# Splitting two products of a Fourier stage once more, and letting ScalarE take casts at any time

## The chip, the cores and the metric

The kernel runs on one core of a Trainium2 chip. The metric is the device time in microseconds, as the median of three runs; the kernel before takes 2945.73 us (2944.1 to 2947.97). One more execution was profiled.

## The reference

Two independent layers whose outputs stand side by side in a 2048 x 2048 result:

```
qkv = x @ wqkv                    # x 2048x1024, wqkv 1024x3072, 32 heads of 32
o = softmax(q k^T / sqrt(32)) v   # for every head
left = o @ wo                     # 2048x1024
a, b = x2 @ Wd_re^T, x2 @ Wd_im^T # first Fourier stage, 1024x1024 matrices
right = Ws_re @ a - Ws_im @ b     # second Fourier stage, 2048x2048 matrices
```

Everything is float32.

## The kernel before, in words

**Arithmetic.** A float32 operand of a projection or Fourier matmul is split into a high part, rounded to TensorE's fast format (`fp32r`), and a low part, the rest. A product of two such operands is three matmuls of 128x128 by 128x512: high-high, low-high and high-low. Each of the large products is cut into 2x2 blocks and done with Strassen's scheme (Winograd's form), seven block products instead of eight, at the price of sums of blocks before and after. `ORDER = (1, 2, 6, 7, 5, 3, 4)` numbers the seven.

**Helpers.** `fetch` loads a block (SyncE issues the DMA) and makes the sums of blocks. `halves` makes the two parts: the cast that makes the high part (line 523 on VectorE, line 522 on ScalarE) and the subtraction that makes the low part (line 526, GpSimd or VectorE). The cast is for VectorE; ScalarE is offered it too only while `spare[0]` is true, which is so in the first five steps of the projection (line 887) and again in the last projection (line 1188), not in attention's time between. `piece` makes a stationary operand, `moving` a moving one. `group` issues the matmuls of one PSUM tile, `gather` reads the finished tile (lines 979 to 1026). An accumulator either stays in SBUF (`Acc`) or travels to HBM and back (`Far`, tiles `x_d`).

**First Fourier stage** (`dense1`). For each of the seven products p there are 8 row blocks i by 2 halves m, and a PSUM tile takes four chunks times three matmuls, 12 in all: 192 matmuls in a product, 1344 in the stage. Rows 0 to 3 accumulate in SBUF, rows 4 to 7 in `x_d`.

**Attention** runs beside these products. For each head, S (line 1317) makes scores for the row maxima: a pair of matmuls into a `psS` tile of 128x1024, VectorE's maximum (line 1323), ScalarE's exponential with sums (line 1326). T (line 1442) makes transposed scores into `psT`, ScalarE's exponential (line 1451) makes `pt`, and V (line 1474) multiplies by the values. `psS` and `psT` have two tiles each.

**Order.** No engine's order is left to a scheduler. `Plan` runs the whole program beforehand with a time for each operation, and writes down an order for each engine. The matmuls of the projections and the Fourier stages ("fills") are one fixed list; S, T and V are three more, and the main loop takes, each time that TensorE is free, the head of one of them by the constants `LATE`, `LEAD`, `STOCK`, `SFIRST` (lines 369 to 378). VectorE, GpSimd, ScalarE and SyncE take what is ready by rank. On the chip each engine then works through its list in order and waits where an input isn't there. The plan lets no GpSimd operation overlap with a VectorE one that has the flag `two`; where a GpSimd operation follows such a one within `Plan.NEAR` (line 79), it is also made to wait for it on the chip.

Of the kernel before, what the change touches and what calls it, by code (L numbers as in the profile page):

```python
# [16 lines left out]
P = 128  # L17
# [48 lines left out]
class Plan:  # L66
# [11 lines left out]
    QUEUE = 1.0  # L78
    NEAR = 0.2

# [140 lines left out]
def kernel(  # L221
# [35 lines left out]
    t2_d = [[dram.tile([P, NB], F32, name=f"t2_d{m}_{k}") for k in range(8)] for m in range(2)]  # L257
    x_d = [[{w: dram.tile([P, NB], F32, name=f"x_d{i}_{m}_{w}") for w in (1, 6, 5)} for m in range(2)] for i in range(4)]
    u4_d = [[dram.tile([P, NB], F32, name=f"u4_d{m}_{i}") for i in range(8)] for m in range(2)]
# [120 lines left out]
    FILL = 3 * (7 * 24 * 4 + 7 * 16 * 4 + 7 * 8 * 16 + 2 * 8 * 4)  # L380
    ATT = H * (128 * MM + 16 * PV) + (3 * H2 + 2 * (H - H2)) * SWITCH
# [81 lines left out]

    def fetch(shape, terms, store=None, keep=None):

        box = {}
        raws, seconds, tile_of, gate = where[0]
        rank = seq()
        sign, *first = terms[0]
        loaded = len(first) == 2  # L470
# [14 lines left out]
        if loaded:  # L485
            last = op("SP", ISSUE, lambda: nc.sync.dma_start(dest(), first[0]), old + first[1] + gate, [users], rank, 256, raws if keep is None else None)
            old = []
        for sign, *term in terms[1:]:
            other = {}
            if len(term) == 2:  # L490
                gold, gusers = seconds.take()

                def load(src=term[0], other=other):
                    other["q"] = tile_of(shape, "g", len(seconds.users))
                    nc.sync.dma_start(other["q"], src)
# [35 lines left out]

    def piece(terms, store=None):

        box = {}
        raw, made, users = fetch([P, 4, P], terms, store)
# [12 lines left out]
        return Piece(h, l, made, both)  # L548
# [9 lines left out]
    def moving(i, terms, store=None, keep=None):  # L558
# [12 lines left out]
        return Piece(h, l, made, mine)  # L571

    whole = lambda t: t

# [41 lines left out]
    def qkv():  # L616
# [269 lines left out]
        for x, (p, blocks, v) in enumerate(STEPS[:10]):  # L886
            spare[0] = x < 5
            if x == 0:
# [67 lines left out]
    def gather(what, X, Y, u3, to, wrote, part=None):  # L956
# [18 lines left out]
        def finish(ps, last):  # L975
# [25 lines left out]
            def put(at, ausers, alast, kind, to, wrote, part):  # L1001
# [20 lines left out]
                if part is not None:  # L1022
                    done = add_op(
                        lambda e: (nc.gpsimd if e == "POOL" else nc.vector).tensor_tensor(out=box["y"], in0=third[0](), in1=box["y"], op=ALU.subtract),
                        [e, third[2]], [users, third[1]], rank)
# [21 lines left out]
    class Far:  # L1047


        def __init__(self, to):  # L1050
            self.to, self.kept, self.last = to, None, None

    FINAL = []
    ab_st = [[[[] for _ in range(NS)] for _ in range(2)] for _ in range(2)]

    def dense1():
# [26 lines left out]
        def load_b(x, n):  # L1083
            p = ORDER[x]
            B[x][n] = moving((8 * x + n) % 12, b_terms(p, n), (t1_d[n], t1[n]) if p == 6 else None)

        B = [[None] * 8 for _ in ORDER]
        for n in range(4):
            load_b(0, n)
        X = {}  # L1090
        for x, p in enumerate(ORDER):
            for i in range(8):
# [19 lines left out]
    def load_ab(step, k):  # L1112
# [10 lines left out]
        }[p]  # L1123
        AB[step, k] = moving((8 * (7 + step) + k) % 12, terms, (t2_d[m][k], t2[m][k]) if p == 6 else None)

    def dense2():
# [3 lines left out]
        for m in range(2):  # L1130
# [13 lines left out]
            for x, p in enumerate(ORDER):  # L1144
                step = 7 * m + x
                for i in range(8):
# [3 lines left out]
                    def terms():  # L1150
                        for k in range(0, 8, 4):
# [4 lines left out]
                            for c in range(4):  # L1156
# [517 lines left out]
```

## Time and profile before

| | |
|---|---|
| median of 3 runs | 2945.73 us |
| profiled execution, whole | 2947.49 us |
| its span, first to last instruction | 2945.7 us |
| TensorE busy, mean granted clock | 2933.7 us, 1.00 |
| VectorE, ScalarE, GpSimd busy | 2300.6, 2271.9, 907.5 us |
| moved by DMA | 588 MB, 200 GB/s |

A matmul's end is modelled, so matmuls overlap in the profile, and a stretch in which TensorE is "busy" can hold waits shorter than a matmul's tail. What one costs is read from a stretch that holds nothing else: its length over the count.

### The profile page before, as it was taken

To read this page: it belongs to the slowest core of one execution; us is meant where nothing else is said; L and a number is where in the kernel's file an instruction comes from. 1 tells how busy PE (TensorE), PEld (TensorE's weight loads), DVE (VectorE), ACT (ScalarE), POOL (GpSimd) and SP (SyncE) were. 2 spreads that over 40 slices of the span, in tenths; PEclk is the share of its full clock that TensorE was granted. 3 is DMA by queue.
4 is the path that set the end of the run, shared out by engine and by line. 5 is a ranking of instruction groups with operands and counts; after the bars stand their busy time and mean duration, and the time that the engine had idled before them with its cause. 6 is when DMAs were issued, how large, how long until landed. Compare 5 with 4: busy or idle time off the path is not lost.

```text
span 2945.7 us, 45665 instructions
## 1 busy us (share of the span) xinstructions
PE 2933.7 (100%) x14922; PEld 2149.6 (73%) x14922; DVE 2300.6 (78%) x3141; ACT 2271.9 (77%) x4321; POOL 907.5 (31%) x709
## 2 busy tenths in 40 slices
PE   9999999999999999999999999999999999999999
PEld 7887777677777777777777777776777766776787
DVE  6778888678877877777678888888777888887685
ACT  4348888888888888888888888888988888886331
POOL 2323336222213332232112543333122444342142
PEclk9999999999999999999999999999999999999999
DMA  9975658667636655665434776565434786655753
GB/s 349 365 237 182 193 184 286 208 214 236 219 109 225 215 177 166 206 231 166 140 111 154 244 230 199 184 195 153 135 112 133 220 264 215 198 179 181 241 201 127
DMA packets 393881, 587.97 MB, mean 200 GB/s; under 512 B 112782, under 2 KB 114574, under 8 KB 393518
## 3 DMA queue, kind: packets, MB, share of 16 engines
q1 hardware_dynamic: 393644, 585.05, 61.8%
q8 instruction: 120, 1.97, 0.3%
q14 instruction: 117, 0.96, 0.1%
HBM read 421.30 MB, written 163.59 MB: 199 GB/s over the span
## 4 chain that ended last, share of the span: by engine, by line
PE 96%; DMA 2%; DVE 1%; SPq 0%; issue 0%; ACT 0%; POOL 0%; DVEq 0%; ACTq 0%
PE pd L416 44%; PE psT L1442 16%; PE psS L1317 16%; PE pd L1474 15%; PE psT L416 6%; DMA qs<-m_d 0%; DVE negm L1323 0%; DMA er<-in_wqk 0%; PE psT L438 0%; DMA g<-in_wqk 0%; DMA raw<-in_wqk 0%; DMA er<-in_xa 0%; DMA g<-in_ct 0%; DMA ks<-qk_d 0%; DVE l L526 0%
## 5 line engine op out<-in xcount | busy, mean ns | idle before, releaser
L1323 DVE TENSOR_REDUCE negm<-psS 128x1 f32<-128x1024 f32 x1024 | 1242.1, 1220 | 239.6 <-PE psS L1317 234.1
L1326 ACT ACTIVATE psS<-psS,negm 128x1024 f32<-128x1024 f32 x1024 | 1219.1, 1190 | 134.3 <-DVE negm L1323 128.7
L416 PE MATMUL pd<-slot,h 128*128 128x512 f32 x3360 | 1147.2, 390 | 0.2 <-DVE ot L1496 0.2
L1451 ACT ACTIVATE pt<-psT 128x512 f32<-128x512 f32 x1296 | 775.0, 695 | 212.5 <-PE psT L1442 201.6
L1442 PE MATMUL psT<-qs,ks 128*128 128x512 f32 x2048 | 793.5, 393 | 1.2 <-DMA qs<-m_d 1.0
L416 PEld LDWEIGHTS pd<-slot,h 128*128 128x128 f32 x3360 | 630.8, 188 | 132.3 <-DVE ot L1496 0.6
L416 PE MATMUL pd<-slot,l 128*128 128x512 f32 x1680 | 654.6, 390 | 0.0
L1317 PE MATMUL psS<-ks,qs 128*128 128x512 f32 x1552 | 473.5, 390 | 1.9 <-ACT psS L1326 1.8
L1442 PEld LDWEIGHTS psT<-qs,ks 128*128 128x128 f32 x2048 | 379.8, 188 | 128.1 <-issue 41.8
L526 POOL TENSOR_TENSOR l<-raw,h 128x512 fp32r<-128x512 f32 x163 | 210.2, 1290 | 728.0 <-PE psT L1442 346.6
L502 POOL TENSOR_TENSOR raw<-raw,g 128x512 f32<-128x512 f32 x225 | 291.9, 1304 | 392.5 <-DVE raw L502 66.2
L416 PEld LDWEIGHTS pd<-slot,l 128*128 128x128 f32 x1680 | 315.4, 188 | 66.8 <-issue 0.8
L1474 PE MATMUL pd<-pt,vt 128*32 128x512 f32 x2592 | 345.8, 594 | 0.4 <-DVE slot L979 0.4
L1317 PEld LDWEIGHTS psS<-ks,qs 128*128 128x128 f32 x1552 | 290.5, 188 | 66.6 <-ACT psS L1326 4.7
L526 POOL TENSOR_TENSOR slot<-raw,slot 128x512 fp32r<-128x512 f32 x174 | 223.8, 1292 | 368.1 <-DVE slot L523 101.5
L1326 ACT ACTIVATION_READ_ACCUMULATOR psS<-psS,negm 128x1 f32 x1024 | 316.6, 309 | 0.0
L1451 ACT ACTIVATE ptm<-psT 128x512 f32<-128x512 f32 x392 | 237.5, 701 | 39.1 <-PE psT L1442 38.4
L1451 ACT ACTIVATE ptl<-psT 128x512 f32<-128x512 f32 x360 | 221.8, 705 | 35.2 <-PE psT L1442 33.2
L1474 PEld LDWEIGHTS pd<-pt,vt 128*32 128x32 f32 x2592 | 89.4, 110 | 180.9 <-issue 173.0
L416 PE MATMUL pd<-slot,slot 128*128 128x512 f32 x768 | 193.7, 390 | 0.0
L416 PEld LDWEIGHTS pd<-slot,slot 128*128 128x128 f32 x768 | 144.2, 188 | 31.0
L523 DVE CAST h<-raw 128x512 fp32r<-128x512 f32 x321 | 148.9, 465 | 16.8 <-PE pd L416 14.2
(138 smaller groups left out, 2362.5 us busy)
## 6 DMA issues: line engine op xcount, KB each, us to landing
raw<-in_ct SPq DMA_DIRECT2D x224, 256.0 KB
g<-in_ct SPq DMA_DIRECT2D x128, 256.0 KB
c<-u_d SPq DMA_DIRECT2D x120, 256.0 KB
qk_d<-e SPq DMA_DIRECT2D x52, 512.0 KB
qs<-qk_d SPq DMA_DIRECT2D x128, 192.0 KB
ks<-qk_d SPq DMA_DIRECT2D x128, 192.0 KB
raw<-ab_d SPq DMA_DIRECT2D x96, 256.0 KB
g<-ab_d SPq DMA_DIRECT2D x80, 256.0 KB
```

Source lines behind the costliest of these rows:

```text
L416: nc.tensor.matmul(box["ps"], a[1]((a[0].hi, a[0].lo)[u]()), b[1]((b[0].hi, b[0].lo)[v]()), start=k == 0, stop=k == n - 1)
L502: return (nc.gpsimd if e == "POOL" else nc.vector).tensor_tensor(out=dest(), in0=dest() if a is None else a.get(), in1=other["q"] if "q" i ...
L523: return nc.vector.tensor_copy(hi(), raw())
L526: return (nc.gpsimd if e == "POOL" else nc.vector).tensor_tensor(out=lo(), in0=raw(), in1=f(hi()), op=ALU.subtract)
L1317: nc.tensor.matmul(p[:, i * NB : i * NB + NB], (QX[0] if own else QS[h % 2])[:, qt * P : qt * P + P], KS[h % 2][:, c * 1024 + i * NB : c * ...
L1323: nc.vector.tensor_reduce(out=ST["negm"][:, c, qt : qt + 1], in_=box["p"], axis=AX.X, op=ALU.max, negate=True)
L1326: nc.scalar.activation(box["p"], box["p"], AF.Exp, bias=ST["negm"][:, c, qt : qt + 1], accum_out=ST["sums"][:, c, qt : qt + 1])
L1442: nc.tensor.matmul(box["p"], KS[h % 2][:, t * P : t * P + P], QS[h % 2][:, j * NB : j * NB + NB], start=True, stop=True)
L1451: nc.scalar.activation(box["t"], box["p"], AF.Exp)
L1474: nc.tensor.matmul(po["p"][j * DH : j * DH + DH, :], VT[h][:, k, :], box["t"], start=(k == t0), stop=(k == t), tile_position=(0, j * DH),)
```

## The change

The products 1 and 2 of the first Fourier stage (`TWICE`) are each split by the same scheme once more: seven products of half the depth, `inner`, in place of eight half-depth ones. The inner sums of blocks are made by `inner_a` and `inner_b`, from the inputs or from tiles kept in HBM (`a2_d`, `b2_d`). The four SBUF accumulators serve the inner products, so all eight rows of the outer ones go through `x_d`. An inner product's stationary operand holds two row blocks by two chunks (`two=True`), its PSUM tile takes 6 matmuls. `turn()` now deals out the 12 slots of moving operands. `spare[0]` is true throughout, and six constants of the plan change.

```
-    NEAR = 0.2            # of Plan
+    NEAR = 0.8
+    b2_d = {p: [dram.tile([P, NB], F32, name=f"b2_d{p}_{c}") for c in range(2)] for p in (1, 2)}
+    a2_d = {p: [dram.tile([P, 4, P], F32, name=f"a2_d{p}_{c}") for c in range(2)] for p in (1, 2)}
+    TWICE, AHEAD = (1, 2), 3
-    LATE = 0.15
+    LATE = 0.05
-    LEAD = 4
+    LEAD = 1
-    STOCK = 1.8
+    STOCK = 1.4
-    SFIRST = 1
+    SFIRST = 0.3
-            spare[0] = x < 5
+            spare[0] = True
...
+        def inner_b(p, q, cc):
+            (sign, at), = OUTER[p][1]
+            r = lambda c2, m: wd[m, 4 * at[0] + 2 * c2 + cc, :, at[1] * NB : at[1] * NB + NB]
+            return {
+                1: lambda: [(1, r(0, 0), [])], 2: lambda: [(1, r(1, 0), [])], 3: lambda: [(1, r(1, 1), [])],
+                5: lambda: [(1, r(0, 1), []), (-1, r(0, 0), [])],
+                6: lambda: [(1, r(1, 1), []), (-1, r(0, 1), []), (1, r(0, 0), [])],
+                7: lambda: [(1, r(1, 1), []), (-1, r(0, 1), [])],
+                4: lambda: [(1, b2_d[p][cc], b2[p][cc]), (-1, r(1, 0), [])],
+            }[q]()
...
+        def inner(x):
+            p = ORDER[x]
+            XI = [a for s in SUMS[:2] for a in accs(s)]
+            YI = [a for s in SUMS[2:] for a in accs(s)]
+            for k, q in enumerate(ORDER):
+                for ip in range(2):
+                    a = piece(inner_a(p, q, ip), (a2_d[p][ip], a2[p][ip]) if q == 6 else None, True)
+                    if ip == 0 and k + AHEAD < 7:
+                        load_inner(x, k + AHEAD)
+                    for il in range(2):
+                        ii = 2 * ip + il
+                        h = DONE.get(q)
+                        to, wrote, part = outer(p, 4 * h[0] + ii, h[1]) if h else (None, None, None)
+                        group(((chunk(a, 2 * il + cc), (B[x][2 * k + cc], whole)) for cc in range(2)), 2, gather(q, XI[ii], YI[ii], None, to, wrote, part))
...
+        for i in range(8):
+            X[i] = [Far(x_d[i][m]) for m in range(2)]
         for x, p in enumerate(ORDER):
+            if p in TWICE:
+                inner(x)
+                continue
```

TensorE's order where product 1 begins. `slot` tiles are moving operands, `h` and `l` a stationary operand's two parts, `pd` PSUM tiles. Before:

```order
L416 MATMUL pd_8889<-slot3_8178,h_8493 128x512
L416 MATMUL pd_8913<-slot4_8600,h_8493 128x512
L1442 MATMUL psT_8923<-qs1_2489,ks1_2490 128x512
L1442 MATMUL psT_8925<-qs1_2489,ks1_2490 128x512
L1317 MATMUL psS_8927<-ks0_530,qx_2491 128x512 x2
L416 MATMUL pd_8913<-slot4_8600,l_8502 128x512
```

The same place after the change:

```order
L419 MATMUL pd_8845<-slot0_7730,h_8506 128x512
L419 MATMUL pd_8845<-slot1_7860,h_8506 128x512
L419 MATMUL pd_8845<-slot1_7860,l_8515 128x512
L419 MATMUL pd_8845<-slot1_7860,h_8506 128x512
L1391 MATMUL psS_8867<-ks1_2523,qs1_2522 128x512 x2
L419 MATMUL pd_8875<-slot0_7730,h_8506 128x512
```

A PSUM tile before takes four slots (`pd_8913` begins on `slot4` and goes on to `slot7`); after, two (`slot0`, `slot1`), and the next tile reads the same two slots again.

TensorE's order toward the end of product 2, before:

```order
L416 MATMUL pd_10421<-slot1_9749,h_9992 128x512
L1317 MATMUL psS_10432<-ks1_2490,qs1_2489 128x512 x2
L1442 MATMUL psT_10436<-qs0_529,ks0_530 128x512
L416 MATMUL pd_10421<-slot1_9749,l_10015 128x512
L1442 MATMUL psT_10441<-qs0_529,ks0_530 128x512
L416 MATMUL pd_10421<-slot1_9749,h_9992 128x512
```

And after the change, 12 fills before that product's end, up to the V that follows (`vt`):

```order
L419 MATMUL pd_10824<-slot3_10272,l_10788 128x512
L419 MATMUL pd_10824<-slot3_10272,h_10748 128x512
L1391 MATMUL psS_10854<-ks0_562,qx_2524 128x512 x2
L1516 MATMUL psT_10867<-qs0_561,ks0_562 128x512
L1516 MATMUL psT_10870<-qs0_561,ks0_562 128x512
L1391 MATMUL psS_10880<-ks0_562,qx_2524 128x512 x2
L1516 MATMUL psT_10885<-qs0_561,ks0_562 128x512
L1516 MATMUL psT_10889<-qs0_561,ks0_562 128x512
L1391 MATMUL psS_10897<-ks0_562,qx_2524 128x512 x2
L1548 MATMUL pd_10906<-pt_10456,vt_8984 32x512
```

Before, fills stand between every S and T; after, the last three S pairs of this piece have T alone between them, since the next fills come behind V.

ScalarE's order in the same stretch, before:

```order
L1326 ACTIVATE psS_10411,sums_9596<-psS_10411,negm_9595 128x1024
L1451 ACTIVATE ptl_10448<-psT_10436 128x512
L1451 ACTIVATE ptl_10454<-psT_10441 128x512
L1326 ACTIVATE psS_10432,sums_9596<-psS_10432,negm_9595 128x1024
L1451 ACTIVATE pt_10476<-psT_10464 128x512
```

And after:

```order
L1400 ACTIVATE psS_10402,sums_9885<-psS_10402,negm_9884 128x1024
L527 ACTIVATE h_10446<-raw_10317 128x512
L1525 ACTIVATE pt_10454<-psT_10419 128x512
L1525 ACTIVATE pt_10456<-psT_10438 128x512
L1400 ACTIVATE psS_10433,sums_9885<-psS_10433,negm_9884 128x1024
L527 ACTIVATE slot4_10474<-raw_10324 128x512
L527 ACTIVATE slot5_10495<-raw_10362 128x512
L1525 ACTIVATE pt_10519<-psT_10512 128x512
```

Casts to high parts (line 527 now) stand between attention's exponentials.

## Rows read from the trace of the kernel before

**Rows 1.** The page: busy time by engine; the chain by engine.
```profile
PE 2933.7 (100%) x14922; PEld 2149.6 (73%) x14922; DVE 2300.6 (78%) x3141; ACT 2271.9 (77%) x4321; POOL 907.5 (31%) x709
...
PE 96%; DMA 2%; DVE 1%; SPq 0%; issue 0%; ACT 0%; POOL 0%; DVEq 0%; ACTq 0%
```

**Rows 2.** TensorE's waits: releaser, us in total, times, longest.
```profile
PE psS L1317 <- ACT psS L1326: 3.0, 3, 1.1
...
PE psT L1442 <- DMA qs<-m_d: 1.0, 2, 0.6
```

**Rows 3.** Fills of line 416 by stretch: stretch, busy (count), clock, DMA, GB/s.
```profile
0.00:793.90 793.90, 519.92 (x1944) 365.00 (x1945) 1.00 0.73 244
793.90:981.10 187.20, 112.30 (x384) 72.12 (x385) 1.00 0.54 171
```

**Rows 4.** All engines by stretch: PE, PEld, DVE, ACT, POOL, clock, DMA, GB/s.
```profile
50.00:100.00 50.00, 50.00 (x222) 41.42 (x221) 36.97 (x46) 19.24 (x32) 19.61 (x15) 1.00 1.02 376
794.00:887.00 93.00, 93.00 (x475) 68.29 (x474) 68.11 (x87) 79.95 (x154) 12.44 (x11) 1.00 0.40 122
887.00:981.00 94.00, 94.00 (x480) 69.62 (x479) 73.62 (x96) 83.12 (x161) 30.48 (x25) 1.00 0.68 220
2300.00:2400.00 100.00, 98.97 (x499) 72.12 (x498) 84.98 (x112) 87.04 (x167) 50.57 (x40) 1.00 0.78 246
2800.00:2900.00 100.00, 100.00 (x443) 82.81 (x442) 88.91 (x121) 34.77 (x58) 45.08 (x35) 1.00 0.58 191
212.00:2755.00 2543.00, 2538.25 (x13192) 1824.50 (x13195) 2006.81 (x2734) 2133.53 (x4092) 793.57 (x618) 1.00 0.60 190
```

**Rows 5.** The page's groups: sums, casts, subtractions, evacuations; busy, mean ns.
```profile
L526 POOL TENSOR_TENSOR l<-raw,h 128x512 fp32r<-128x512 f32 x163 | 210.2, 1290 | 728.0 <-PE psT L1442 346.6
...
L523 DVE CAST h<-raw 128x512 fp32r<-128x512 f32 x321 | 148.9, 465 | 16.8 <-PE pd L416 14.2
```

**Rows 6.** The groups of ScalarE and VectorE, shapes kept apart.
```profile
L526 DVE TENSOR_TENSOR l<-raw,h 128x512 fp32r<-128x512 f32 x158 | 112.8, 719 | 3.1
...
L1019 DVE TENSOR_TENSOR e<-c,pd 128x512 f32<-128x512 f32 x85 | 57.8, 680 | 9.7 <-PE pd L416 8.3 <-DMA g<-ab_d 0.4
...
L522 ACT ACTIVATE slot<-raw 128x512 fp32r<-128x512 f32 x57 | 35.6, 631 | 86.8 <-DMA raw<-in_wo 20.1 <-DVE raw L502 19.2 <-PE psT L416 17.7
```

**Rows 7.** In order of time, 1645 to 1654 us: start, us, engine, line.
```profile
1645.94 0.62 PE L1317 MATMUL psS<-ks,qs 128*128 128x512 f32 x2
...
1646.20 1.20 ACT L1326 ACTIVATE psS<-psS,negm 128x1024 f32<-128x1024 f32 x1
...
1646.59 1.22 DVE L1323 TENSOR_REDUCE negm<-psS 128x1 f32<-128x1024 f32 x1 [0.62 <-PE psS L1317]
...
1647.29 1.21 ACT L1451 ACTIVATE pt<-psT 128x512 f32<-128x512 f32 x2
...
1647.60 5.78 POOL L502 TENSOR_TENSOR raw<-raw,g 128x512 f32<-128x512 f32 x4 [1.39 <-DMA raw<-ab_d]
1647.73 1.44 DVE L523 CAST h<-raw 128x512 fp32r<-128x512 f32 x1
...
1648.24 1.23 ACT L1326 ACTIVATE psS<-psS,negm 128x1024 f32<-128x1024 f32 x1
...
1649.21 1.67 DVE L526 TENSOR_TENSOR l<-raw,h 128x512 fp32r<-128x512 f32 x1
1649.24 0.35 ACT L1326 ACTIVATION_READ_ACCUMULATOR psS<-psS,negm 128x1 f32 x1
...
1650.02 0.62 PE L1317 MATMUL psS<-ks,qs 128*128 128x512 f32 x2
...
1652.11 1.09 ACT L1326 ACTIVATE psS<-psS,negm 128x1024 f32<-128x1024 f32 x1 [1.55 <-DVE negm L1323]
...
1653.37 0.73 PE L1317 MATMUL psS<-ks,qx 128*128 128x512 f32 x2 [1.15 <-ACT psS L1326]
```

More of the change, by code (lines that the diff above doesn't have):

```diff
@@ L257 @@
     t2_d = [[dram.tile([P, NB], F32, name=f"t2_d{m}_{k}") for k in range(8)] for m in range(2)]
-    x_d = [[{w: dram.tile([P, NB], F32, name=f"x_d{i}_{m}_{w}") for w in (1, 6, 5)} for m in range(2)] for i in range(4)]
+    x_d = [[{w: dram.tile([P, NB], F32, name=f"x_d{i}_{m}_{w}") for w in (1, 6, 5)} for m in range(2)] for i in range(8)]
     u4_d = [[dram.tile([P, NB], F32, name=f"u4_d{m}_{i}") for i in range(8)] for m in range(2)]
@@ L468, in fetch @@
         rank = seq()
+        square = (lambda t: t.rearrange("p (i c) m -> p i c m", i=2)) if two else whole
         sign, *first = terms[0]
@@ L485, in fetch @@
         if loaded:
-            last = op("SP", ISSUE, lambda: nc.sync.dma_start(dest(), first[0]), old + first[1] + gate, [users], rank, 256, raws if keep is None else None)
+            last = op("SP", ISSUE, lambda: nc.sync.dma_start(square(dest()), first[0]), old + first[1] + gate, [users], rank, 256, raws if keep is None else None)
             old = []
@@ L514 @@
     spare = [True]
+    whole = lambda t: t
     def halves(raw, made, users, hi, lo, old, mine, order=(None, None)):
@@ L530, in halves, with piece @@
         return a, b
-    def piece(terms, store=None):
+    def piece(terms, store=None, two=False):
         box = {}
-        raw, made, users = fetch([P, 4, P], terms, store)
+        raw, made, users = fetch([P, 4, P], terms, store, None, two)
         (o0, u0), (o1, u1) = HR.take(), LR.take()
@@ L571, in moving @@
         return Piece(h, l, made, mine)
-    whole = lambda t: t
     def chunk(p, c):
@@ L1023, in put @@
                     done = add_op(
-                        lambda e: (nc.gpsimd if e == "POOL" else nc.vector).tensor_tensor(out=box["y"], in0=third[0](), in1=box["y"], op=ALU.subtract),
+                        lambda e: (nc.gpsimd if e == "POOL" else nc.vector).tensor_tensor(out=box["y"], in0=third[0](), in1=box["y"], op=part[2]),
                         [e, third[2]], [users, third[1]], rank)
@@ L1051, in __init__, with turn @@
             self.to, self.kept, self.last = to, None, None
+    turns = [0]
+    def turn():
+        turns[0] += 1
+        return (turns[0] - 1) % 12
     FINAL = []
@@ L1084, in load_b @@
             p = ORDER[x]
-            B[x][n] = moving((8 * x + n) % 12, b_terms(p, n), (t1_d[n], t1[n]) if p == 6 else None)
-        B = [[None] * 8 for _ in ORDER]
+            if p in TWICE:
+                if n == 0:
+                    for q in range(AHEAD):
+                        load_inner(x, q)
+                return
+            B[x][n] = moving(turn(), b_terms(p, n), (t1_d[n], t1[n]) if p == 6 else None)
+        def inner_b(p, q, cc):
[8 more added lines that the diff above has]
+            }[q]()
@@ new lines, in load_inner, with outer @@
+        def load_inner(x, k):
+            p, q = ORDER[x], ORDER[k]
+            for cc in range(2):
+                B[x][2 * k + cc] = moving(turn(), inner_b(p, q, cc), (b2_d[p][cc], b2[p][cc]) if q == 6 else None)
+        def outer(p, i, m):
+            to = X[i][m].to[1] if p == 1 else ab_d[m][DONE[p][1]][8 * DONE[p][0] + i]
+            wrote = [] if p == 1 else ab_st[m][DONE[p][1]][8 * DONE[p][0] + i]
+            part = None if p == 1 else (*X[i][m].kept, ALU.add)
+            if p == 1:
+                X[i][m].kept = to, wrote
+            return to, wrote, part
@@ new lines, in inner @@
+        def inner(x):
[12 more added lines that the diff above has]
+                        group(((chunk(a, 2 * il + cc), (B[x][2 * k + cc], whole)) for cc in range(2)), 2, gather(q, XI[ii], YI[ii], None, to, wrote, part))
+                    if k > 4:
+                        for n in range(2 * (k - 5) + ip, 2 * (k - 5) + ip + 1):
+                            load_b(x + 1, n)
@@ L1164, in dense2 @@
                         gather(p, X[i // 2][i % 2], None, (u4_d[m][i], u4[m][i]), to,
-                               [] if m else y_st[t][e], (y_d[t][e], y_st[t][e]) if m and h else None),
+                               [] if m else y_st[t][e], (y_d[t][e], y_st[t][e], ALU.subtract) if m and h else None),
                     )
```

27 lines of the change are left out of this document (20 added, 7 removed).

## The prediction

> **What bounds the kernel now.** I read the page's busy times and its chain first [rows 1]. TensorE is busy for 2933.7 of 2945.7 us, and 96% of the chain that ended last is TensorE's own. VectorE and ScalarE are at 78% and 77%, GpSimd at 31%. So 12.0 us are idle on TensorE in the whole program, and the reader is to see that nothing but its instruction count, and what is in those 12 us, can be saved. Since a busy TensorE can hide short waits, I then asked how fast matmuls follow one another where nothing else runs: in 2800 to 2900 us there are 443 matmuls of 512 columns in 100 us, that is 0.2257 us each, at a granted clock of 1.00, the 2.4 GHz level; 50 to 100 us gives 222 in 50 us, the same figure [rows 4]. Everywhere else the clock is the same, so a matmul that goes is worth 0.2257 us wherever it stood.
>
> Next the place. Counting fills of line 416, 1944 stand before 793.9 us (with 72 of line 438, by the code, they are the projection's 2016), and 384 = 2 x 192 in 793.9 to 981.1 us [rows 3]: these 187 us are the first two products, the stretch that the change rewrites. There TensorE is busy throughout, VectorE for 68.1 + 73.6 = 141.7 us, ScalarE for 163.1, GpSimd for 42.9, and DMA moves 122 and 220 GB/s [rows 4]. TensorE's list of waits tells which wait ends last: the largest inside attention is for ScalarE's exponential to free a `psS` tile, 3.0 us in three waits; that for the maxima's way through HBM is 1.0 us [rows 2].
>
> **The change, part by part.**
>
> *Matmuls.* Each of the two products goes from 192 to 7 x 2 x 2 x 6 = 168 matmuls. 48 x 0.2257 = 10.8 us go from TensorE, with nothing to hide that gain, since TensorE has no other bound here.
>
> *What is paid for it.* Counted from the code for both products: 24 more operands to split (a cast and a subtraction each), 40 sums of blocks, 32 more evacuations, 16 sums of a second outer result with the first one's. That is 136 elementwise operations. Of them the evacuations are VectorE's alone, 32 x 0.680 = 22 us. The 80 others besides casts cost 0.72 us on VectorE or 1.29 on GpSimd [rows 5, 6], 58 to 103 us. The stretch has 45 us free on VectorE and 144 on GpSimd. As the new lists have it, over the whole program VectorE gets 108 fewer casts, 8 fewer copies and 46 more sums and subtractions, near 50 + 6 - 32 = 24 us less; GpSimd gets 74 operations more, 74 x 1.29 = 95 us; ScalarE 132 casts, 132 x 0.631 = 83 us. Between 212 and 2755 us ScalarE is busy for 2133.5 of 2543 us [rows 4], so it has 410 us for them. All of this lies beside TensorE's work: no engine reaches its limit, and I cost it at nothing directly.
>
> *DMAs.* 136 more transfers of 256 KB: 88 in the two products, and 48 later, because rows 0 to 3 now travel through `x_d` too. In the stretch 171 GB/s over 187.2 us are 32.0 MB now [rows 3]; 88 x 0.262 = 23.1 MB come on top, and the stretch is 176 us long, so it asks for 313 GB/s. The trace shows 376 GB/s in 50 to 100 us [rows 4]. It fits, with a sixth to spare, and SyncE's queue holds 136 issues more, each ahead of loads that later fills need; what this costs if it doesn't fit is the slower rival below.
>
> *The order.* Smaller `LATE`, `LEAD`, `STOCK` and `SFIRST` place S and T differently everywhere. In TensorE's new order S and T stand between fills as regularly as before, but for one place: at the end of product 2 the fills run out ahead of a V, and three S pairs follow with only T between them. From the first of these pairs to the third, which needs the same `psS` tile, there are 8 matmuls, 8 x 0.2257 = 1.8 us. What must happen in between is shown by an undisturbed pair [rows 7]: the pair starts at 1645.94, the maximum at 1646.59 for 1.22 us, and an exponential from 1648.24 to the end of its accumulator's read at 1649.59 is 1.35; 0.65 + 1.22 + 1.35 = 3.2, some 3.3 us with the hand-overs. That forces a wait of 1.5 us. If ScalarE is late there already, its own rhythm decides: an exponential of S and two of T take 1648.24 - 1646.20 = 2.04 us, two rounds 4.1, and the wait is 2.3. I take 2.0 us for this place, between the two, as its S pairs come just after dense ones. Nothing queued behind it gains from the wait but ScalarE.
>
> *A cast in front of an exponential.* ScalarE's new list has casts among attention's exponentials. One holds the next exponential for 0.63 us. The undisturbed pair has 1650.02 - 1649.59 = 0.43 us to spare, so a cast at a bad moment costs TensorE 0.2 us, at a good one nothing; 132 of them bound it between 0 and 26 us. I take 0, because the plan put them where it found ScalarE free, and the operation has the same duration in the plan and on the chip, 0.63 us; the other end is part of the rivals.
>
> *VectorE and GpSimd.* What a wait inside attention comes from is shown in rows 7: a late `ab_d` block lets GpSimd do four sums on end, 1647.60 to 1653.38; beside them a cast takes 1.44 us instead of 0.465 on average, a subtraction 1.67 instead of 0.72 [rows 5, 6], the maximum starts late, the exponential 1.55 us late, and TensorE stands for 1.15 us. Fewer casts on VectorE and the wider `Plan.NEAR` make this rarer: at best all 3.0 us of rows 2 go. More sums on GpSimd, at a higher DMA load, make it likelier: 2300 to 2400 us has GpSimd at 51%, 246 GB/s and 1.0 us idle on TensorE [rows 4], and the rewritten stretch will have more of both, for 176 us: two or three such events of 1.2 us, 3.6 at most. Between -3.0 and +3.6 I take 0.
>
> The Trainium skill's page "SBUF — State Buffer" (section "SBUF: two separate sides") says that VectorE and GpSimd share a pair of ports as an exclusive lock: whoever starts first keeps it for its whole instruction, where VectorE has two inputs from SBUF or runs in a two-port mode, and the other stands still. The stretched cast and subtraction of rows 7 agree with that; how long the lock was held no row shows. By that rule alone the 74 added operations on GpSimd speak against the change, and the 108 casts that leave VectorE for it, so it moves no term.
>
> *The sum.* The profiled execution took 2947.49 us, 1.8 us more than its span. 2947.5 - 10.8 + 2.0 = 2938.7. It is 1.8 us above the median of the runs, 2945.73, so the median to expect is 2936.9, that is 2937.
>
> **The rivals.**
>
> *The lists run better than before.* For it: the casts off VectorE, and 4.0 us of waits in rows 2 that aren't bound to any stretch. Against it: the new place without fills. With the waits of rows 2 down by 3.0 us the time is 2934.
>
> *The new stretch drifts.* GpSimd, at 42.9 of 187 us there [rows 4], goes to (42.9 + 55 x 1.29) / 176 = 65% if 55 of its 74 new operations fall there, VectorE and ScalarE come close to full, and the lists leave little room to catch up in. For it: the mechanism of rows 7. Against it: the plan keeps VectorE and GpSimd apart. With five events of 1.2 to 1.3 us the gain shrinks by 6.3: 2943.
>
> *DMA can't bring the inputs (slower).* Its place is the same stretch. Without fills TensorE has attention alone, whose round of 2.04 us on ScalarE holds only four matmuls, 0.90 us, so 56% of such time is lost. 55.1 MB have to come; at 313 GB/s they just do. If the queue moves 260 GB/s there, a little above the 246 of 2300 to 2400 us [rows 4], they need 212 us instead of 176: 36 us without fills, 20 us lost, 2957. It turns slower by over 0.2% where 14.8 us are lost, that is 26 us of drought, below 273 GB/s. Against it: 376 GB/s were moved at the start.
>
> *The change doesn't do what it says* can't be for the matmuls, which are counted; for ScalarE's casts it would leave the forecast as it is.
>
> **How the numbers follow.** The forecast has 0.46, with a range of its own from 2935 to 2940 (the wait of 1.5 to 2.3 us, and a few events more or fewer). The better lists have 0.22, the drift 0.23, DMA 0.09. Two tenths of a per cent, 5.9 us, are about what a measurement of this kernel can tell from no change. Faster than 2939.8 is nearly all of the first two, 0.65; slower than 2951.6 is DMA's case, 0.08; the rest, 0.27, is the same. The range that leaves out 2 in 10 reaches from 2932 into the drift's case, to 2946.
>
> **What would show it.** Right: TensorE busy for about 10.8 us less, with 48 matmuls fewer at 0.2257 us; the two products' fills in some 178 us; one gap of about 2 us ahead of a V near 945 us, ended by ScalarE's exponential; no wait of TensorE's for an input from DMA in the stretch; ScalarE's busy time up by 83 us, GpSimd's by 95. Wrong: waits of fills for `l` or `slot` tiles made by GpSimd, a DMA share near 1.00 over the stretch, or VectorE's casts and sums stretched far over 0.47 and 0.72 us there. A granted clock under 1.00 after a gap would also upset the count.

## The result, and the profile after

| | before | after |
|---|---|---|
| median, in runs side by side | 2945.49 us (2942.06 to 2949.61, 8 runs) | 2952.97 us (2949.45 to 2955.34, 8 runs) |
| profiled execution, its span | 2947.49, 2945.7 us | 2953.48, 2951.7 us |

The ratio is 1.0023, 95% interval 1.0014 to 1.0032: slower by 7.5 us, where 2937 was predicted. All spans below are of the one profiled execution of a kernel, all medians of five executions or more. An execution can lie 4 us or more from its kernel's median (e10's profiled one does), so a trace tells where time goes, and a median how much. The section on the change speaks of six constants of the plan; five are edited (`NEAR`, `LATE`, `LEAD`, `STOCK`, `SFIRST`).

Busy times and the chain of the kernel after, against [rows 1]:

```profile
PE 2934.1 (99%) x14874; PEld 2136.2 (72%) x14874; DVE 2288.3 (78%) x3073; ACT 2339.5 (79%) x4451; POOL 998.8 (34%) x783
...
PE 94%; DMA 3%; DVE 1%; ACT 1%; SPq 0%; POOL 0%; issue 0%; DVEq 0%; ACTq 0%; POOLq 0%
```

The 48 matmuls are gone (14922 to 14874), yet TensorE is busy for 0.4 us more: what they saved has come back inside "busy". DMA's share of the chain goes from 2 to 3%, ScalarE's from 0 to 1%. TensorE's waits in the kernel after (releaser, us in total, times, longest), against [rows 2]:

```profile
PE psS L1391 <- ACT psS L1400: 5.7, 8, 1.3
PE psT L1516 <- DMA qs<-m_d: 3.1, 3, 1.5
...
PE pd L419 <- POOL l L531: 0.8, 1, 0.8
```

S's waits for an exponential went from 3.0 to 5.7 us, those for the maxima's way through HBM from 1.0 to 3.1, and a fill waits for a subtraction of GpSimd's. Fills of line 419 by stretch (PE, PEld, clock, DMA, GB/s), against [rows 3]:

```profile
0.00:786.00 786.00, 518.67 (x1944) 365.01 (x1944) 1.00 0.74 248
786.00:970.00 184.00, 99.68 (x336) 62.87 (x337) 1.00 0.84 271
```

and all engines (PE, PEld, DVE, ACT, POOL, clock, DMA, GB/s), against [rows 4]:

```profile
786.00:875.00 89.00, 88.27 (x448) 60.81 (x450) 79.13 (x113) 78.64 (x152) 52.75 (x42) 1.00 0.80 258
875.00:965.00 90.00, 86.94 (x462) 58.11 (x453) 79.63 (x116) 76.98 (x149) 59.79 (x48) 1.00 0.87 282
2800.00:2900.00 100.00, 100.00 (x443) 82.80 (x442) 87.02 (x120) 32.52 (x54) 45.08 (x35) 1.00 0.61 209
```

The two products take 184 us for 336 fills, where they took 187.2 for 384. In the 179 us from 786 to 965, VectorE is at 89%, GpSimd at 63%. Where nothing else runs, matmuls follow one another as before. Of the 443 that a window of 100 us counts, 441 start in it, so that the spacing is 0.2267 us rather than the 0.2257 of the prediction; 48 matmuls are 10.9 us rather than 10.8.

**A view that shows what "busy" hides.** From each kernel's trace I took the intervals between the starts of consecutive TensorE matmuls (V behind V apart), summed what each has above 0.226 us, and parted them at 60 ns: longer ones are waits, the switch to V's shape, or matmuls at half the clock (below); shorter ones are matmuls that follow a few ns late. The steady spacing of 226.7 ns itself puts some 7 us into each sum up to 60 ns, so that only differences between the rows count. The sums hold to 0.3 us.

| sums in us | up to 60 ns | over 60 ns | span |
|---|---|---|---|
| before | 16.5 | 49.1 | 2945.7 |
| after | 23.7 | 58.9 | 2951.7 |
| e6, LATE alone | 22.9 | 48.8 | 2951.9 |
| e13, LATE for attention alone | 21.4 | 48.6 | 2950.4 |
| e14, LATE for fills alone | 15.8 | 45.8 | 2941.9 |
| e15, LATE 0.2 | 14.2 | 44.7 | 2939.0 |
| e7, after with LATE 0.15 | 19.7 | 63.6 | 2952.7 |
| e10, e7 with thinner loads | 19.2 | 52.4 | 2940.9 |

For after this gives 7.2 + 9.8 - 10.9 = +6.1 against a span longer by 6.0 us. So two losses are to be explained: 7.2 us in small delays, 9.8 us in waits.

Matmuls at half the clock are in some of these sums. In the profiles of e1, e2, e7, e11 and e12 the granted clock is 0.5, the 1.2 GHz level, for a few us once or twice inside the program, each time behind intervals of 2.1 to 4.5 us between two matmuls, and the next matmuls follow one another by 0.427 us. (Intervals of 2.2 us in e8 and e10 were followed by none.) Twenty us that hold such a place (PE, PEld, DVE, ACT, POOL, clock, DMA, GB/s), in e1 and in e7:

```profile
1040.00:1060.00 20.00, 16.21 (x65) 12.97 (x65) 12.47 (x16) 13.82 (x26) 2.58 (x3) 0.91 0.72 210
980.00:1000.00 20.00, 17.56 (x87) 10.85 (x90) 13.88 (x18) 17.27 (x33) 7.27 (x6) 0.91 1.03 368
```

Each place costs 1.5 to 2 us on top of its gap. Before, after and the profiles of the other runs have none until the program's last few us, so neither after's loss nor that of `LATE` below is the clock's. Executions that weren't profiled can have such places: their mean granted clock is on record, and where it is 0.999 or less their times are mostly the longer ones.

### The profile page after: what moved, and what is told of

Its sections match the earlier page's. It is cut to its first block, busy times and chain, and to the rows that moved or that the text cites. A ratio compares the mean times of both kernels' runs of the same rounds, so it can differ in the third digit from the quotient of the medians.

```text
span 2951.7 us, 46199 instructions
## 1 busy us (share of the span) xinstructions
PE 2934.1 (99%) x14874; PEld 2136.2 (72%) x14874; DVE 2288.3 (78%) x3073; ACT 2339.5 (79%) x4451; POOL 998.8 (34%) x783
## 4 chain that ended last, share of the span: by engine, by line
PE 94%; DMA 3%; DVE 1%; ACT 1%; SPq 0%; POOL 0%; issue 0%; DVEq 0%; ACTq 0%; POOLq 0%
PE pd L419 42%; PE psT L1516 16%; PE psS L1391 15%; PE pd L1548 14%; PE psT L419 6%; DMA raw<-in_xb 1%; ACT psS L1400 0%; DMA qs<-qk_d 0%; DMA er<-in_wv 0%; DVE negm L1397 0%; DMA qk_d<-e 0%; DMA qs<-m_d 0%; DMA er<-in_xa 0%; DMA raw<-in_wd 0%; PE psT L441 0%
## 5 line engine op out<-in xcount | busy, mean ns | idle before, releaser
L1400 ACT ACTIVATE psS<-psS,negm 128x1024 f32<-128x1024 f32 x1024 | 1231.6, 1203 | 67.6 <-DVE negm L1397 65.3
L1525 ACT ACTIVATE pt<-psT 128x512 f32<-128x512 f32 x1296 | 790.4, 705 | 180.8 <-PE psT L1516 171.4
L506 POOL TENSOR_TENSOR raw<-raw,g 128x512 f32<-128x512 f32 x258 | 331.3, 1292 | 378.3 <-DMA raw<-in_ct 47.9
L531 POOL TENSOR_TENSOR l<-raw,h 128x512 fp32r<-128x512 f32 x185 | 238.5, 1290 | 630.1 <-PE psT L1516 288.0
L531 POOL TENSOR_TENSOR slot<-raw,slot 128x512 fp32r<-128x512 f32 x182 | 234.3, 1293 | 489.7 <-DVE slot L528 170.4
L1400 ACT ACTIVATION_READ_ACCUMULATOR psS<-psS,negm 128x1 f32 x1024 | 329.9, 322 | 0.0
L1391 PE MATMUL psS<-ks,qx 128*128 128x512 f32 x496 | 150.8, 395 | 2.5 <-ACT psS L1400 2.5
```

What stands on the lines that cost most here:

```text
L506: return (nc.gpsimd if e == "POOL" else nc.vector).tensor_tensor(out=dest(), in0=dest() if a is None else a.get(), in1=other["q"] if "q" i ...
L531: return (nc.gpsimd if e == "POOL" else nc.vector).tensor_tensor(out=lo(), in0=raw(), in1=f(hi()), op=ALU.subtract)
L1391: nc.tensor.matmul(p[:, i * NB : i * NB + NB], (QX[0] if own else QS[h % 2])[:, qt * P : qt * P + P], KS[h % 2][:, c * 1024 + i * NB : c * ...
L1400: nc.scalar.activation(box["p"], box["p"], AF.Exp, bias=ST["negm"][:, c, qt : qt + 1], accum_out=ST["sums"][:, c, qt : qt + 1])
L1525: nc.scalar.activation(box["t"], box["p"], AF.Exp)
```

## The experiments

The theories, by letter: **A**, inputs come late in the rewritten stretch; **B**, a cast on ScalarE holds up the exponential behind it; **C**, the new constants leave the lists without slack; **D**, by `LATE` 0.05 the `psS` and `psT` tiles come free just ahead of the matmul that needs them, and the following matmuls are late by a few ns. E and F are named where they come up.

### Split or constants?

Run e1 has the split with the old constants and casts:

```
-    NEAR = 0.8 ... LATE = 0.05 ... LEAD = 1 ... STOCK = 1.4 ... SFIRST = 0.3 ... spare[0] = True
+    NEAR = 0.2 ... LATE = 0.15 ... LEAD = 4 ... STOCK = 1.8 ... SFIRST = 1 ... spare[0] = x < 5
```

> The two products split again, but the constants of the plan and ScalarE's casts as before the change. Theory A (in the rewritten stretch inputs land later than their place in the lists, VectorE and GpSimd stand behind them, and a maximum behind those is late): it carries the loss alone, so 2946 to 2956 us with 6 us or more of waits on TensorE between 786 and 1000 us. Theory B (ScalarE's casts hold up exponentials) and theory C (LATE, LEAD, STOCK and SFIRST leave the lists without slack): both causes are gone, so 2945.5 - 10.8 + 2 for the gap of the plan, 2935 to 2940 us.

Measured: 2954.87 us, ratio 1.0024 (1.0014 to 1.0035), as slow as after. Its small delays are near those of before (17.7 us), its intervals over 60 ns sum to 67.3, of which some 1.9 are matmuls at half the clock. A's range and sign came true; B and C, which had 2935 to 2940, aren't needed for a loss of this size.

Run e2 is the kernel after with `spare[0] = x < 5` again:

> The changed kernel with ScalarE's casts as before the change. Theory A: the stretch keeps its waits of about 10 us, and VectorE has 100 casts more there and elsewhere, so 2951 to 2958 us. Theory B: the waits for ScalarE outside the stretch and most of those in it go, 2938 to 2943 us. Theory C: no change, 2950 to 2955 us.

Measured: 2963.34, ratio 1.0056 (1.0043 to 1.0069). Without ScalarE's casts the split kernel is 10 us slower: B is not what makes it slow. Some 3.6 us of the 10 are matmuls at half the clock in the profiled execution, behind two gaps, at 338 and 1046 us; the time is also above A's range.

Run e3 is the kernel before with all five constants and the casts, without the split:

> The kernel before with the new constants and ScalarE's casts at any time, without the split: 48 matmuls more than the changed kernel. Theory A: only the waits outside the stretch stay, which grew by about 6 us, so 2945 to 2952 us, and none of the 10 us between 786 and 1000 us. Theory B or C: the waits come with the casts or the constants, so 2955 to 2964 us.

Measured: 2953.52, ratio 1.0023 (1.0014 to 1.0032). A loss of the same size is there without the split, at a time that no theory had forecast: above A's range, below that of B and C. With the same constants, 48 matmuls fewer gain nothing that can be told from noise (each kernel is at 1.0023 of the kernel before beside it): the split pays its own 10.9 us back too.

Run e4 is the kernel after with the first term alone of each inner sum of blocks; it leaves out 40 loads and 40 sums:

```
-    a = piece(inner_a(p, q, ip), ...)
+    a = piece(inner_a(p, q, ip)[:1], ...)    # and inner_b(p, q, cc)[:1]
```

> The changed kernel, but each inner operand is its first block alone: the other terms of the inner sums are left out, that is 40 loads of 256 KB and 40 sums less in the two products; the matmuls, casts and accumulations are as in the changed kernel. Theory A: the waits between 786 and 1000 us fall from about 10 us to under 4, 2943 to 2948 us. Theory B or C: the waits stay, 2950 to 2955 us.

Measured: 2948.28, ratio 1.0006 (0.9997 to 1.0015), 4.7 us under after, just above A's range. A's sign, waits under 4 us in the stretch, did not come true. From 940 to 1020 us the DMA engines are still full and TensorE idles 4.7 us:

```profile
940.00:1020.00 80.00, 75.26 (x382) 49.95 (x382) 68.68 (x93) 67.79 (x130) 41.26 (x33) 1.00 0.97 321
```

Over 786 to 1020 us intervals over 60 ns sum to 9.0 us, against 10.4 in after; most of the gain lies behind 1020 us, where the edit changes nothing but the lists. So this run doesn't price the loads and sums that it leaves out.

### Which constant?

Run e5 is e3 with `LATE = 0.15`; e6 is the kernel before with one edit:

```
-    LATE = 0.15
+    LATE = 0.05
```

> The kernel of e3 (no split, new constants, casts on ScalarE) with LATE back at 0.15 alone. Theory D (with LATE at 0.05 tiles of psS and psT come free under 0.3 us ahead of the matmul that takes them, and the next matmuls follow by 231 to 236 ns instead of 226, 25 ns in all after each): the 6.8 us of matmul intervals stretched by up to 60 ns that e3 has over before go, 2945 to 2949 us, stretched intervals near 17 us in sum as before. Theory B (ScalarE's casts) or the other constants: 2952 to 2955 us as e3.

> The kernel before with LATE at 0.05, nothing else. Theory D: stretched intervals sum to about 23 us instead of 16.5, 2950 to 2955 us. Theory B or the other constants: no change, 2943 to 2949 us.

Measured: e5 2950.34, ratio 1.0011 (1.0003 to 1.002); e6 2953.32, ratio 1.0022 (1.0013 to 1.0031), 6.5 us over the kernel before beside it. In the kernel before, this one number of the plan makes a loss of the size of e3's. It doesn't come back whole: with `LATE` at 0.15 again, e5 keeps 3.5 of e3's 6.6 us and lies above D's range, though its small delays are near those of before, 18.3 us. Four of its eleven executions have a mean granted clock of 0.999 and took 2952.57 to 2953.83; the seven at 1.000 took 2946.07 to 2950.55. `LEAD` and `Plan.NEAR` had no run of their own.

The stretch from 1000 to 2600 us shows how `LATE` costs time, first in before, then in e6:

```profile
1000.00:2600.00 1600.00, 1596.27 (x8303) 1150.34 (x8302) 1267.51 (x1699) 1355.81 (x2609) 502.47 (x391) 1.00 0.58 182
```

```profile
1000.00:2600.00 1600.00, 1595.68 (x8284) 1146.96 (x8283) 1255.53 (x1683) 1361.31 (x2618) 505.55 (x393) 1.00 0.58 180
```

V's share is the same in both (282.9 us). TensorE is busy as long, to 0.6 us, and gets 19 matmuls fewer done, 4.3 us. What such a place looks like, in order of time in e6 (start, us, engine, line):

```profile
1239.05 1.10 ACT L1451 ACTIVATE pt<-psT 128x512 f32<-128x512 f32 x2
...
1239.96 0.39 PE L1442 MATMUL psT<-qs,ks 128*128 128x512 f32 x1
...
1240.19 0.19 PEld L1442 LDWEIGHTS psT<-qs,ks 128*128 128x128 f32 x1
1240.42 0.40 PE L1442 MATMUL psT<-qs,ks 128*128 128x512 f32 x1
...
1241.58 0.62 PE L1317 MATMUL psS<-ks,qs 128*128 128x512 f32 x2
```

The exponentials that free the `psT` tile end at 1240.15. The weight load of the T that needs it starts at 1240.19, and the T at 1240.42, 0.27 us behind the release. From the T at 1239.96 to the S at 1241.58 there are seven intervals of 0.231 us. No row shows a wait. Counted behind 800 us in before: where T's tile came free 0.15 to 0.275 us ahead, the seven intervals around it are longer by 20 ns in sum, at 0.325 to 0.5 us by 2 ns. T's tile was free less than 0.3 us ahead 164 times in before, 426 times in e6: 262 more at some 20 ns are 5 us, an estimate, of the 6.4 by which the small delays grew.

Runs e7 and e8 are the kernel after with `LATE = 0.15` and `LEAD = 4`, e7 also with `AHEAD = 4`:

> The changed kernel with LATE back at 0.15, LEAD back at 4, and the inner moving operands loaded four products ahead instead of three. Theory D with A (late inputs in the rewritten stretch): the stretched intervals fall to 17 to 18 us and the waits of the stretch shrink too, since loads start one inner product, some 12 us, earlier: 2938 to 2946 us. If the operands come late for another reason than the start of their loads, the stretch keeps its 10 us and the time is 2944 to 2949 us. Theory B: 2950 to 2955 us.

> As e7, but loaded three products ahead as in the changed kernel. Theory D: the stretched intervals fall to 17 to 18 us; what the lists do with the stretch is open, since with LATE at 0.15 matmuls are put behind operands that come later; 2944 to 2952 us. Theory B: 2950 to 2955 us. Against e7 it tells what loading earlier is worth.

Measured: e7 2952.93, ratio 1.0018 (1.0009 to 1.0027); e8 2957.47, ratio 1.0032 (1.002 to 1.0045). Both lie above D's ranges: `LATE` can't simply be put back under the split. Small delays fall (19.7 us in e7), and intervals over 60 ns grow by as much; some 3.3 us of these are matmuls at half the clock, at 341 and 986 us. The profiled execution of e8, the only one of five with a mean granted clock of 1.000, took 2949.93 us, the others 2956.09 to 2959.46 at 0.998 or 0.999; no trace shows those.

### Where the split loses its own gain

In after, the waits cluster at the end of product 2 and the start of product 6. The intervals over 60 ns once more, without those beside a V, parted at 786 and 1020 us:

| sums in us | 786 to 1020 us | elsewhere |
|---|---|---|
| before | 0.8 | 19.7 |
| after | 10.4 | 20.3 |
| e1, split with the old constants | 16.6 | 21.6 |
| e3, no split | 0.8 | 19.7 |
| e4, first terms alone | 9.0 | 15.3 |
| e7, after with `LATE` 0.15 | 9.2 | 26.3 |
| e9, after with thinner loads | 6.7 | 19.4 |
| e10, e7 with thinner loads | 4.6 | 19.5 |
| e12, product 1 alone split | 2.2 | 27.0 |

Of after's 9.8 us more, 9.6 are in these 234 us, and they come with the split of both products, under the new constants (after) and the old ones (e1). DMA in 940 to 1020 and 980 to 1000 us, before:

```profile
940.00:1020.00 80.00, 80.00 (x418) 58.04 (x417) 65.35 (x90) 68.92 (x134) 28.17 (x23) 1.00 0.71 227
980.00:1000.00 20.00, 20.00 (x122) 12.49 (x121) 16.25 (x22) 14.51 (x28) 9.52 (x8) 1.00 0.86 285
```

and after:

```profile
940.00:1020.00 80.00, 76.53 (x394) 52.58 (x392) 70.32 (x96) 69.37 (x133) 45.30 (x37) 1.00 0.99 336
980.00:1000.00 20.00, 18.31 (x83) 13.58 (x85) 17.63 (x21) 17.15 (x34) 10.21 (x8) 1.00 1.00 350
```

For 80 us the DMA engines are full, and TensorE idles 3.5 us. A full queue doesn't always cost it anything: from 1000 to 1020 us the share is 1.03, at 361 GB/s, and TensorE doesn't idle. How a full queue reaches TensorE, in order of time in after:

```profile
981.74 2.41 SPq L499 DMA_DIRECT2D g<-in_xb  x2
...
983.33 0.61 PE L1391 MATMUL psS<-ks,qs 128*128 128x512 f32 x2
...
985.30 0.69 DVE L506 TENSOR_TENSOR raw<-raw,g 128x512 f32<-128x512 f32 x1 [2.37 <-DMA g<-in_xb]
...
985.91 1.22 DVE L1397 TENSOR_REDUCE negm<-psS 128x1 f32<-128x1024 f32 x1
...
987.23 1.09 ACT L1400 ACTIVATE psS<-psS,negm 128x1024 f32<-128x1024 f32 x1 [1.36 <-DVE negm L1397]
...
988.48 0.73 PE L1391 MATMUL psS<-ks,qs 128*128 128x512 f32 x2 [0.92 <-ACT psS L1400]
```

A sum waits 2.37 us on VectorE for its second term; the maximum of the S pair of 983.33 stands behind it in VectorE's list and starts 2 us late; the exponential is late by 1.36, the next S pair by 0.92. Here the fills' operands weren't late; attention was, behind a sum that was. (One fill of the stretch did wait, 0.8 us at 991 us, for an `l` of GpSimd's.)

Run e9 thins the loads and keeps every instruction: 76 second and third terms in the first three products fetch a quarter of their bytes, which the sum reads four times over (the values change). Run e10 does that to e7.

```
-    nc.sync.dma_start(square(other["q"]), src)
+    nc.sync.dma_start(blocks(other["q"])[:, 0:1], (src[:, 0:1, 0] if two else blocks(src)[:, 0:1]))
...
```

> The changed kernel, in which the 72 loads of a second or third term of a sum of blocks (tile g) in the first three products fetch a quarter of their bytes, 64 KB for 256, and the sum reads that quarter four times over: the right output's values are left wrong. Instructions, their order and the planned times are those of the changed kernel. Theory A, now put as 'the DMA queue is full at the end of product 2': the changed kernel has a DMA share of 1.00, 0.92, 1.00 and 1.03 in the four 20-us pieces from 940 to 1020 us, where the kernel before has 0.77, 0.64, 0.86 and 0.59, and TensorE's waits stand just there; with some 14 MB fewer the share falls to about 0.8, the waits of 980 to 1000 us (2.0 us) go and those of 940 to 960 us (2.6 us) shrink to the 1.5 us that eight matmuls between two S pairs force: 2947 to 2950. Theory E, 'the sums and casts themselves are too many for VectorE, GpSimd and ScalarE there': nothing changes, 2952 to 2954. Theory D (LATE) says nothing of this stretch; its 6 us stay in.

> The kernel of run e7 (the changed one with LATE 0.15, LEAD 4, AHEAD 4) with the same 72 loads cut to a quarter. Theory A with D: both costs are away, the waits of 900 to 1000 us in e7 (7.2 us) fall to 2 or less, and at last most of the 10.8 us of 48 matmuls shows: 2944 to 2948. Theory E: as e7, 2952 to 2954. If e9 gains and this one doesn't, the waits of e7 that stand elsewhere (S pairs behind ScalarE's exponential, 3.0 us at 341 us, 1.2 to 1.6 us at 1308 and 1688 us) are what LATE 0.15 costs beside the new lists.

Measured: e9 2950.19, ratio 1.0009 (1.0 to 1.0018), 2.8 us under after; e10 2947.18, ratio 1.0 (0.9992 to 1.0009), 5.8 under e7. The stretch in e9, then in e10:

```profile
940.00:1020.00 80.00, 78.22 (x404) 54.94 (x403) 70.99 (x98) 71.44 (x139) 44.34 (x35) 1.00 0.89 283
980.00:1000.00 20.00, 20.00 (x120) 13.38 (x122) 17.34 (x24) 17.65 (x35) 9.66 (x9) 1.00 0.88 280
```

```profile
940.00:1020.00 80.00, 79.04 (x407) 55.38 (x406) 70.25 (x94) 72.28 (x141) 44.70 (x36) 1.00 0.90 285
```

VectorE and GpSimd do as much as before the thinning, and the waits of 980 to 1000 us are gone. That speaks for theory A in the form "the queue is full", against E, "too many sums and casts", which had no change. The shares fell to 0.89, not 0.8 as expected, and e9 is just outside the range that A gave it; its interval touches that of after, and e10, inside its range, is the clearer of the two. In the stretch from 786 to 1020 us, thinner loads take 3.7 us of waits from after and 4.6 from e7, of which some 1.6 were matmuls at half the clock. What is left there, 6.7 and 4.6 us, they don't explain.

Run e12 splits product 1 alone (`TWICE = (1,)`):

> The changed kernel with product 1 alone split; product 2 is the 192 matmuls of before, so 24 matmuls fewer in all, 5.4 us. LATE 0.05 and the other constants as in the change. Theories A and D: the queue isn't full where an ordinary product 2 lies between the split one and product 6, so the 6.3 us of LATE less 5.4 us are left, with 0 to 2 us of waits: 2946.5 to 2949. Theory E: each split product costs what it saves, 2951 to 2954.

Measured: 2957.41, ratio 1.003 (1.0019 to 1.0042). A miss for A and D in the time, though not in the stretch:

```profile
940.00:1020.00 80.00, 80.00 (x418) 57.87 (x417) 62.78 (x83) 69.74 (x135) 28.95 (x23) 1.00 0.80 267
```

TensorE is full there, as A says. The time went elsewhere. Small delays are 7.6 us over before, as in after. A T waits 2.6 us for `m_d` near 1280 us. And in the last projection the changed lists put casts that the program's end waits for:

```profile
2797.33 0.49 PE L419 MATMUL psT<-slot,slot 128*128 128x512 f32 x1 [3.74 <-ACT slot L527]
...
2799.15 1.22 PE L419 MATMUL psT<-slot,slot 128*128 128x512 f32 x2 [1.33 <-DVE slot L531]
```

These two waits are 5.1 us, and behind this place and the one near 1280 us matmuls at half the clock cost 3.1 us more. Each edit writes all lists anew, and such places come and go with them. E, by which each split product costs what it saves, isn't borne out for product 1: of the 5.4 us saved it costs 1.4 in the stretch.

Run e11 is the kernel before with `STOCK = 1.4`, `SFIRST = 0.3` and the casts, `LATE` as it was:

> The kernel before with STOCK 1.4, SFIRST 0.3 and ScalarE's casts allowed throughout, but LATE 0.15, LEAD 4 and Plan.NEAR 0.2 as before; no split. Theory D: without LATE 0.05 nothing is lost, 2944 to 2947.5. Theory C (STOCK and SFIRST leave the lists without slack): 2949 to 2952. Theory B (a cast in front of an exponential): up to 2 or 3 us over the kernel before, with waits of S pairs behind ScalarE, 2947.5 to 2949.

Measured: 2948.84, ratio 1.0007 (0.9998 to 1.0016). No loss that can be told from none, though the median is above D's range and in B's; one wait of 3.6 us stands out, at 341 us, and some 1.6 us of matmuls at half the clock follow it:

```profile
338.22 0.69 DVE L502 TENSOR_TENSOR raw<-raw,g 128x512 f32<-128x512 f32 x1 [4.84 <-DMA raw<-in_wqk]
338.83 1.22 DVE L1323 TENSOR_REDUCE negm<-psS 128x1 f32<-128x1024 f32 x1
...
340.14 1.09 ACT L1326 ACTIVATE psS<-psS,negm 128x1024 f32<-128x1024 f32 x1 [4.04 <-DVE negm L1323]
...
341.40 0.80 PE L1317 MATMUL psS<-ks,qs 128*128 128x512 f32 x2 [3.62 <-ACT psS L1326]
```

It is the mechanism of 985 us again, and not a cast's: a sum on VectorE ahead of its transfer, a maximum behind it.

### Theory D from both sides

Run e13 is the kernel before with `LATE` 0.05 for S, T and V alone; e14 with 0.05 for the first fill of a PSUM tile alone. Rival F: the loss is the fills'. Run e15 goes the other way:

```
-    LATE = 0.15   STOCK = 1.8   SFIRST = 1
+    LATE = 0.2    STOCK = 1.4   SFIRST = 0.3
-            if ready + (LATE if first else 0.0) <= pl.now:
+            if ready + (0.15 if first else 0.0) <= pl.now:
```

> The kernel before with 0.05 for 0.15 where LATE holds back S, T and V; the first matmul of a PSUM tile of fills keeps 0.15. Theory D (psS and psT tiles that come free less than 0.3 us ahead of their matmul, which then delays the weight load and stretches the next few matmuls to 230 to 237 ns): all of the loss of run e6, 6.4 us, is here, in intervals that are longer by under 60 ns; the small ones sum to 22 to 24 us (16.5 in the kernel before): 2951 to 2954. Rival F (the loss comes from fills that begin as soon as their operands or PSUM tile are there): 2945.5 to 2948.

> The other half: S, T and V keep 0.15, the first matmul of a PSUM tile of fills has 0.05. Theory D: nothing is lost, 2945.5 to 2948, small intervals 16 to 18 us. Rival F: the loss of e6 is here, 2951 to 2954.

> The other direction, a candidate to beat both kernels: 0.2 for S, T and V, 0.15 for fills, with STOCK 1.4 and SFIRST 0.3, no split, ScalarE's casts as before. Theory D: in the kernel before some 240 tiles of S and T come free under 0.3 us ahead of their matmul and cost near 3 us in small intervals; with more slack these fall to 13 to 15 us, and if no new wait comes, the time is 2943 to 2946. If slack is dear elsewhere (S and T later, ScalarE's exponentials and VectorE's maxima with less to catch up in), waits over 130 ns grow by as much: 2946 to 2950.

Measured: e13 2951.39, ratio 1.0019 (1.0011 to 1.0028); e14 2945.01, ratio 0.9998 (0.9989 to 1.0007); e15 2941.87, ratio 0.9987 (0.9978 to 0.9996). The stretch of e6 above, in e13, e14 and e15:

```profile
1000.00:2600.00 1600.00, 1595.82 (x8290) 1147.98 (x8289) 1255.12 (x1686) 1360.62 (x2620) 504.55 (x394) 1.00 0.58 180
```

```profile
1000.00:2600.00 1600.00, 1597.58 (x8314) 1153.10 (x8313) 1266.77 (x1701) 1358.33 (x2612) 500.91 (x390) 1.00 0.58 182
```

```profile
1000.00:2600.00 1600.00, 1598.26 (x8328) 1156.61 (x8327) 1259.77 (x1699) 1363.55 (x2622) 514.17 (x401) 1.00 0.58 182
```

8303 matmuls before, 8290 with less slack for attention, 8314 with less for fills, 8328 with more for attention. F falls. D holds in both directions, with e14 and e15 a little faster than it forecast, and small delays a little smaller in e13 and e14 (21.4 and 15.8 us): in e15 tiles of T that come free under 0.3 us ahead fall from 164 to 55. With 3.6 us under the kernel before beside it, e15 is the fastest kernel of this study, without the split. Of its shorter span, 2.3 us are small delays and 4.4 are in intervals over 60 ns; how much of the latter is `LATE`, and how much `STOCK` and `SFIRST`, was not parted. (e11, with the same two at `LATE` 0.15, has small delays of 17.6 us.)

## Why the prediction was wrong

The profiled execution took 2953.48 us where the sum gave 2938.7, which is 14.8 us too low. The sum had 0 for small delays, which grew by 7.2, and 2.0 for waits, which grew by 9.8. Two steps failed.

*Matmuls.* Right: 48 fewer. The spacing was read 0.4% too short, which moves nothing.

*The order: the first step that failed.* It said of the smaller `LATE`, `LEAD`, `STOCK` and `SFIRST` only that S and T stand between fills as regularly as before, and so costed them at nothing. The place in the list is not all: `LATE` sets how long, in the plan, a tile has been free when its matmul starts. In the kernel before, that term measured +6.5 us (e6), +5.9 for attention alone (e13); in after, small delays are 7.2 us over before, and in e1, with `LATE` at 0.15, 1.2. That 6.5 is near the 7.5 between the kernels is so because the split's gain of 10.9 and its waits of 9.8 nearly cancel. The rows that the prediction read could not show the term: [rows 4] count S, T, V and fills together, and call the delays busy.

*What is paid for the split: the second step.* Operations and loads were costed at nothing "directly", with 2.0 us for one gap and 0 for events. From 786 to 1020 us there are 9.6 us more of waits instead, and 15.8 in e1, so they don't hang on `LATE` at 0.05.

*The gap at the end of product 2.* Right in size, at 953 us for "near 945". The S pairs with T alone between them, in order of time in after:

```profile
948.04 0.73 PE L1391 MATMUL psS<-ks,qs 128*128 128x512 f32 x2 [0.59 <-ACT psS L1400]
...
954.25 0.73 PE L1391 MATMUL psS<-ks,qx 128*128 128x512 f32 x2 [0.59 <-ACT psS L1400]
...
956.32 0.73 PE L1391 MATMUL psS<-ks,qx 128*128 128x512 f32 x2 [0.59 <-ACT psS L1400]
956.34 1.39 ACT L1400 ACTIVATE psS<-psS,negm 128x1024 f32<-128x1024 f32 x1
```

The pairs stand 2.07 us apart, the rhythm of ScalarE that was worked out as 2.04; the intervals from 953 to 957 us are 1.9 us too long, for 2.0 predicted. The place wasn't the only one: the pair of 948.04 too has T alone ahead of it, and 0.8 us were lost there.

*DMAs.* Wrong: "it fits, with a sixth to spare" is true of the stretch as a whole (271 GB/s over 184 us, for 313 asked) and not of the 80 us around its end, with the loads of product 6, where the share is 0.99. The sign that was named, a share near 1.00 over the stretch, was therefore too coarse; over the stretch it was 0.84. The slower rival, with a chance of 0.09, named the queue, but a drought of fills, at 260 GB/s. What came is a queue that is full at 336 GB/s, and sums that stand waiting ahead of maxima; thinning the loads gives 2.8 us back in e9, 5.8 in e10.

*ScalarE's casts, VectorE and GpSimd.* ScalarE's busy time rose by 67.6 us and GpSimd's by 91.3, for 83 and 95 predicted; VectorE's fell by 12.3, for 24. No run shows a cost of the casts, and without them (e2) the split is 10 us worse.

*What stays open.* Of the 9.6 us more of waits from 786 to 1020 us, 2.7 are the two places with T alone between S pairs, and 3.7 went with thinner loads in e9. The other 3 or so us stand there too, and no run tells their cause. Nor do the runs show why e5, e7 and e8, with `LATE` back at 0.15, keep a loss: part of it is in executions with a granted clock under 1.00, of which there are few traces.

## What to carry to other kernels

Where a list is planned ahead, the slack between a tile's release and its next use is a cost term, though no row shows a wait: compare the number of matmuls in equal stretches, not their busy time. An edit that writes all lists anew moves waits everywhere: look at the stretch that it was meant for before its time is taken for an answer. Bandwidth is to be summed over the densest stretch of the queue, the start of the next stage included, not over the stage that is rewritten. A sum that may wait for a transfer, placed ahead of an operation on the path, hands its wait on.

## What was not expected of the hardware

A matmul whose PSUM tile came free 0.15 to 0.275 us before its start does not only start late: the seven intervals around it were 20 to 30 ns longer in sum (T and S in before), in steps of 4 to 10 ns, and by 2 ns where the tile had been free for 0.325 us or more. Why a release acts on several later matmuls the runs don't show.

Behind an interval of 2.1 to 4.5 us without a new matmul, TensorE's granted clock was 0.5 for a few us in five of the profiles, at 0.427 us a matmul, so that a single late operand costs more than its wait: in e11 3.6 us of wait and 1.6 us behind it.
